# A GraphSAGE layer with sorted edges: nine buffers instead of five for the gathered leftover rows, and up to nine rows ahead

## The chip, the cores and the metric

The kernel runs on one core of a Trainium2 chip. The core has five engines with a queue each, which work side by side and wait for each other by semaphores: TensorE (PE in the profile, PEld for its weight loads), VectorE (DVE), ScalarE (ACT), GpSimd (POOL) and SyncE (SP, which here only issues transfers). Every engine takes its own instructions strictly in the order in which they stand. A transfer (DMA) is issued by an engine and then runs by itself.

The metric is the device time of one execution in microseconds (us), taken as the median of several runs. Less is better.

## What is computed

One layer of a graph network over 12500 nodes and 800000 random edges, 64 features each: every node sums the features of its neighbours, scales the sum, and two small weight matrices are applied.

```python
N, deg, D = 12500, 64, 64
E = N * deg
...
nsum = _segment_sum(x[src], dst, N)
h_neigh = nsum * deg_inv[:, None]
return x @ w_self + h_neigh @ w_neigh
```

`src` and `dst` are the two ends of each edge, drawn at random.

## The kernel before

The kernel sorts the edges itself. Each edge becomes one 32-bit key, made of its destination group, its source block of 128 nodes and the places inside both. The keys are sorted in 128 separate runs, one to a partition (DVE, line 230). Then rows of equal keys are cut out of the runs and merged, in two parts: part 0 holds the lower 37 buckets of each row, part 1 the upper 23. The cutting is done by `gather_runs` (line 394): one indirect DMA of POOL for each of 128 runs, followed by one or two short memsets of POOL that only pass time (`pause`, line 307). The merge (`merge_runs`) works on the tile `u`. It takes the runs in blocks of 32; for each block its first step copies on ACT (line 421) and compares on DVE (line 416), and needs all gathers of that block; further steps are at line 456. The three blocks of part 1 are `(0, 2), (2, 1), (3, 1)`: runs 0 to 63, 64 to 95 and 96 to 127.

The second half of the program is `nodes`. It goes through 7644 buckets (blocks, counted by `b0`), eight to a tile, in the order of destination groups; six groups of 98 blocks make an octet of 588 blocks, which shares one pair of accumulators. For each tile:

- `one_hots` makes, for 28 blocks at a time, two matrices of zeros and ones on DVE, `ohs` for the sources (line 838, three buffers) and `ohd` for the destinations (line 841, five buffers), from the lists `slb` that SP loads;
- PE multiplies `ohs` with the features `xh`, which picks the source rows into `ct` (line 867); ACT, and DVE for some tiles, copy them to `xg` (lines 877 and 875);
- two tiles later PE multiplies `xg` with `ohd` into the accumulators (line 923, in `sums`).

A bucket holds at most 128 edges that way. The few edges that don't fit are the leftovers: 140 lists of 128 edges. `uses` gives for each list the block at which it is added in. In the first octet all eight lists are added near its end, at blocks 404, 428, 452 and so on to 572. `rest(b0)`, called ahead of each tile's sums, does up to three things:

- it issues the indirect DMA that gathers a list's 128 source rows into a buffer `lx` (line 887, on POOL; at most one for each call);
- it makes the list's one-hot matrix `ohl` (line 895, DVE), with five buffers and at most five ahead;
- it multiplies the two into the accumulators (line 903, PE) once the block is reached.

A row load may be placed when fewer than five loaded lists are unused at that point of the program, and when its use is at most 400 blocks away (160 from near the first octet's end on). The buffer of a new load is that of the list five places earlier, so POOL waits until PE has used it.

The order of all this is the order of the program's text: from `after_sort` on no scheduler moves anything. `sums_and_merge` steps through the tiles of `nodes` by a counter `n` and puts other work between them: at every third `n` one of the last 32 gathers of part 1 (`runs`, numbers 96 to 127); from `n` = 8 on steps of the merge, as many as an allowance of 420 ns a tile pays for. The last block of the merge, which needs those 32 gathers, is not begun before `n` = 100 (`RESUME`). When the merge is done, part 1 is searched and decoded, and its leftovers follow. At the end of each octet `finish` writes the output (DMA at line 994 on POOL's queue, after DVE at lines 992 and 993).

Of the kernel before, what the change touches and what calls it, by code (L numbers as in the profile page):

```python
# [13 lines left out]
FH = mybir.dt.float16  # L14
# [54 lines left out]
READY = 8  # L69
SLOT = 1250  # L70
OCT = 6
LEAST = 2 * HN * NDB
LEND = 14

# [187 lines left out]
class Kernel:  # L262
# [497 lines left out]
    def tail(self, mps):  # L760
# [25 lines left out]
        for c in range(n):  # L786
# [3 lines left out]
                in_offset=bass.IndirectOffsetOnAxis(ap=s[:, c:c + 1].bitcast(U32), axis=0))  # L790
        m = pool.tile([128, n, N - LEAST], FH, name="tm")
        for c in range(n):
            if c % 4 == 0:
                yield
            nc.vector.tensor_scalar(m[:, c], self.wide[:, :N - LEAST], z[:, c:c + 1], -float(LEAST),
                                    op0=OP.subtract, op1=OP.is_equal)
        yield
        yield
        yield
        ps = mps.tile([128, N - LEAST], F32, name="tps", tag="ct", bufs=3)  # L800
        for c in range(n):
            nc.tensor.matmul(ps, rows[:, c], m[:, c], start=c == 0, stop=c == n - 1)
        g = pool.tile([128, N - LEAST], F32, name="tg")
        nc.scalar.activation(g, ps, AF.Copy)
# [5 lines left out]
    def uses(self):  # L810


        out = []
        for o in range(0, NBID, OCT * NB):
            end = min(o + OCT * NB, NBID)
            here = []
# [27 lines left out]
    def nodes(self, pool, aps, mps):  # L844


        nc = self.nc
        source = self.one_hots(pool)
        ready = []
        pend = []  # L850
        late = []
        done = []
        acc = own = None
        uses = self.uses()
        picked, ohl = [], []
        turn = 0

        def gather(b0, cnt, vector):

            nonlocal turn  # L860
            ct = aps.tile([128, 1024], F32, name="ct", bufs=3)
            while len(ready) < min(cnt + AHEAD, NBID - b0):
                ready.extend(next(source))
            cols = ready[:cnt]
            del ready[:cnt]
            for i in reversed(range(cnt)):
                nc.tensor.matmul(ct[:, i * 128:(i + 1) * 128], cols[i][0],  # L867
                                 self.xh[:, (b0 + i) % NB].rearrange("p a f -> p (a f)"), start=True, stop=True)
            xg = pool.tile([128, 1024], FH, name="xg", bufs=7)
            if vector and len(ready) < min(8 + AHEAD, NBID - b0 - cnt):  # L870
                turn += 1
            else:
                vector = False
            if vector and turn % 2:
                nc.vector.tensor_copy(xg[:, :cnt * 128], ct[:, :cnt * 128])  # L875
            else:
                nc.scalar.activation(xg[:, :cnt * 128], ct[:, :cnt * 128], AF.Copy)  # L877
            return b0, xg, [d for _, d in cols]

        def rest(b0):  # L880

            early = 400 if b0 < OCT * NB - 160 else 160
            if len(picked) < self.used + 5 and len(picked) < len(uses) and uses[len(picked)][0] - early <= b0 \
                    and uses[len(picked)][1] in self.left:
                _, p, c, _, _ = uses[len(picked)]
                x = pool.tile([128, 128], FH, name="lx", bufs=5)
                nc.gpsimd.indirect_dma_start(  # L887
                    out=x, out_offset=None, in_=self.xt,
                    in_offset=bass.IndirectOffsetOnAxis(ap=self.left[p][1][:, c:c + 1], axis=0))
                picked.append(x)  # L890
                self.picked = len(done)
            if len(ohl) < len(picked) and len(ohl) < self.used + 5 and uses[len(ohl)][0] - 96 <= b0:
                _, p, c, first, end = uses[len(ohl)]
                m = pool.tile([128, 4 * HN], FH, name="ohl", bufs=5)
                nc.vector.tensor_scalar(m[:, :(end + 1 - first) * 2 * HN], self.wide[:, :(end + 1 - first) * 2 * HN],
                                        self.left[p][0][:, c:c + 1], -float(first * 2 * HN),
                                        op0=OP.subtract, op1=OP.is_equal)
                ohl.append(m)
            while self.used < len(uses) and uses[self.used][0] <= b0:
                _, p, c, first, end = uses[self.used]  # L900
                m = ohl[self.used].rearrange("p (b h n) -> p b h n", h=2, n=HN)
                for h in range(2):
                    nc.tensor.matmul(acc[h][:, first % OCT * HN:(first % OCT + end + 1 - first) * HN],  # L903
                                     picked[self.used], m[:, :end + 1 - first, h], start=False, stop=False)
                self.used += 1

        def sums(job):

            nonlocal acc
            b0, xg, cols = job  # L910
            o = b0 // (OCT * NB)
            end = min((o + 1) * OCT * NB, NBID)
            last = b0 + len(cols) == end
            nb = min(OCT, NDB - o * OCT)
            width = nb * HN
            if b0 % (OCT * NB) == 0:
                acc = [aps.tile([128, OCT * HN], F32, name=f"acc{h}", bufs=1) for h in range(2)]
            rest(b0)
            for i, d in enumerate(cols):
                db, sb = divmod(b0 + i, NB)  # L920
                for h in range(2):
                    r = slice(h * H, (h + 1) * H)
                    nc.tensor.matmul(acc[h][:, db % OCT * HN:(db % OCT + 1) * HN], xg[r, i * 128:(i + 1) * 128], d[r],  # L923
                                     start=db % OCT == 0 and sb == 0, stop=b0 + i + 1 == end)
            if last:
                g = self.fin.tile([128, OCT, 2, HN], F32, name="g", bufs=1)
                for h in range(2):
                    nc.scalar.activation(g[:, :nb, h], acc[h][:, :width].rearrange("p (b n) -> p b n", n=HN), AF.Copy)
                g = g.rearrange("p b h n -> p (b h n)")
                for q in range(2):  # L930
                    if (2 * o + q) * 4 * FB < N:
                        late.append([b0 + 40 * (1 + 3 * q), self.finish(2 * o + q, g[:, q * 4 * FB:(q + 1) * 4 * FB],
                                                                        self.fin, mps, self.w2n, own and own[q])])
            return last

        tiles = []
        for o in range(0, NBID, OCT * NB):
            end = min(o + OCT * NB, NBID)
            tiles += [(b0, min(8, end - b0)) for b0 in range(o, end, 8)]
        for t, (b0, cnt) in enumerate(tiles):  # L940
            pend.append(gather(b0, cnt, t >= SHARE))
            if t % 2:
                while len(pend) > 2:
                    if sums(pend.pop(0)):
                        break
            if late and b0 >= late[0][0]:
                if next(late[0][1], self) is self:
                    late.pop(0)
                else:
                    late[0][0] = b0 + 40  # L950
            if t == len(tiles) - 12:
                own = [self.load_own(NQ - 3 + q, self.fin) for q in range(2)]
            done.append(t)
            yield t
        for job in pend:
            sums(job)
        for _, f in late:
            for _ in f:
                pass
# [270 lines left out]
```

## Time and profile before

| What | us |
| --- | --- |
| median of 3 runs | 1882.71 |
| lowest and highest run | 1881.04, 1889.39 |
| the profiled execution's time | 1888.32 |
| its span in the profile | 1886.6 |
| DVE busy | 1667.2 (88%) |
| ACT busy | 1169.7 (62%) |
| PE busy | 980.7 (52%) |
| POOL busy | 809.9 (43%) |
| POOL's row loads (line 887), 140 of them | 231.2 busy, 261.6 idle before them |
| POOL's gathers of runs (line 394), 256 of them | 374.0 busy, 178.8 idle before them |

How to read the rows of the profile that follow. A row of the timeline gives the start in us, the length in us, the engine, the line, the operation, what it writes and reads, how many instructions are merged in the row, and in brackets how long the engine stood idle before it and what ended that ("issue" where nothing that the profile shows did). A row of the waits says which instruction waited for which, with the sum in us, the number of times and the longest. A row of the stretches gives the window, its length, the busy time of each engine with the number of instructions, the granted clock of PE (1.00 is full), the busy share of the DMA engines and GB/s.

### The profile page before, as it was taken

How to read it: one execution, taken by the hardware profiler on the slowest of the kernel's cores; microseconds unless marked ns; L12 is line 12 of the kernel's file. 1: busy time of each engine (PE TensorE's matmuls, PEld its weight loads, DVE VectorE, ACT ScalarE, POOL GpSimd, SP SyncE). 2: the span in 40 equal slices, each digit the busy share in tenths (PEclk: the TensorE clock that was granted, in tenths of full speed). 3: DMA queues.
4: the chain of work that ended last, by engine and by line, in shares of the span. 5: the costliest groups of instructions: out<-in, count | busy, mean ns of one | idle time of the engine just before them, and what ended most of it. 6: DMA issues, size and time to landing. Idle time of an engine off the chain costs nothing.

```text
span 1886.6 us, 54681 instructions
## 1 busy us (share of the span) xinstructions
PE 980.7 (52%) x23698; PEld 839.0 (44%) x23698; DVE 1667.2 (88%) x1805; ACT 1169.7 (62%) x1868; POOL 809.9 (43%) x917
## 2 busy tenths in 40 slices
PE   0015100000000000185888888888868989988997
PEld 0003100000000000174777777777757778777886
DVE  6999999999559999797799999998897888888885
ACT  7435128206500032485898888889977877877786
POOL 1000000798889986888713131313552142222321
PEclk9998655555555555598899999999999999999999
DMA  4304100011100012476678877779766888788784
GB/s 153 70 0 100 36 32 7 21 35 38 22 19 9 10 45 79 127 267 194 211 228 240 264 238 262 244 253 329 264 203 228 267 274 264 253 277 254 247 261 144
DMA packets 104805, 305.25 MB, mean 162 GB/s; under 512 B 52945, under 2 KB 60491, under 8 KB 103915
## 3 DMA queue, kind: packets, MB, share of 16 engines
q1 hardware_dynamic: 86347, 277.44, 41.7%
q0 software_dynamic: 17632, 22.17, 8.8%
q8 instruction: 187, 3.06, 0.6%
q10 hardware_dynamic: 576, 2.07, 0.3%
q14 instruction: 63, 0.52, 0.1%
HBM read 282.20 MB, written 19.41 MB: 160 GB/s over the span
## 4 chain that ended last, share of the span: by engine, by line
DVE 42%; PE 25%; POOL 13%; issue 10%; ACT 5%; DMA 4%; DVEq 0%; SPq 0%; ACTq 0%; POOLq 0%
DVE u L456 15%; PE ct L867 13%; POOL u L394 10%; PE acc L923 9%; DVE b L230 6%; DVE a L230 6%; DVE ohd L841 6%; DVE ohs L838 4%; DMA slb<-sl 2%; ACT xg L877 2%; POOL pad L307 2%; POOL lx L887 1%; DVE u L416 1%; PE acc L903 1%; POOL v L620 1%
## 5 line engine op out<-in xcount | busy, mean ns | idle before, releaser
L877 ACT ACTIVATE xg<-ct 128x1024 f16<-128x1024 f32 (+1 forms) x898 | 852.2, 1033 | 187.3 <-PE ct L867 154.8
L867 PE MATMUL ct<-xh,ohs 128*128 128x128 f16 x7644 | 545.4, 224 | 80.3 <-DVE ohs L838 40.0
L867 PEld LDWEIGHTS <-ohs 128*128 128x128 f16 x7644 | 450.2, 100 | 125.6 <-issue 64.2
L394 POOL DMA_INDIRECT u<-d,ix x256 | 374.0, 1461 | 178.8 <-DVE ix L386 135.4
L923 PE MATMUL acc<-ohd,xg 64*128 64x80 f16 x15288 | 405.9, 199 | 64.2 <-issue 48.9
L456 DVE TENSOR_TENSOR u<-u 128x1456 f32<-128x1456 f32 (+51 forms) x314 | 398.1, 1291 | 19.7 <-ACT u L421 13.6
L923 PEld LDWEIGHTS <-xg 64*128 64x128 f16 x15288 | 319.7, 96 | 135.0 <-issue 65.2
L841 DVE TENSOR_TENSOR ohd<-iota,dlT 128x2240 f16<-128x2240 bf16 x273 | 359.8, 1318 | 0.0
L838 DVE TENSOR_SCALAR ohs<-slb,pidx 128x3584 f16<-128x3584 bf16 x273 | 314.7, 1153 | 35.1 <-PE ct L867 16.6
L887 POOL DMA_INDIRECT lx<-xt,lsrc x140 | 231.2, 1652 | 261.6 <-PE acc L903 228.4
L230 DVE TENSOR_TENSOR b<-a 128x608 f32<-128x608 f32 (+44 forms) x124 | 173.8, 1444 | 6.3 <-ACT a L232 2.3
L230 DVE TENSOR_TENSOR a<-b 128x608 f32<-128x608 f32 (+44 forms) x124 | 173.9, 1445 | 4.5
L994 POOL DMA_DIRECT2D out<-o x25 | 23.7, 949 | 339.6 <-DVE o L993 257.6
L384 PE MATMUL stp<-idf,st 128*128 128x128 f32 x2 | 0.9, 445 | 310.7 <-DVE st L382 310.7
L677 PE MATMUL tr<-idb,l 128*128 128x128 bf16 x60 | 8.0, 273 | 263.9 <-ACT l L671 253.2
L384 PEld LDWEIGHTS stp<-idf,st 128*128 128x128 f32 x2 | 0.4, 183 | 311.1 <-issue 311.1
L875 DVE CAST xg<-ct 128x1024 f16<-128x1024 f32 x64 | 78.2, 1223 | 68.3 <-PE ct L867 63.5
L677 PEld LDWEIGHTS <-l 128*128 128x128 bf16 x60 | 4.9, 117 | 267.1 <-ACT l L671 255.7
L421 ACT ACTIVATE u<-u 128x96 f32<-128x96 f32 (+36 forms) x155 | 32.9, 258 | 134.3 <-DVE u L456 71.1
L375 ACT ACTIVATE junka<-b,c 128x132 bf16<-128x132 f32 (+46 forms) x205 | 90.8, 443 | 12.3 <-DVE b L230 5.8
L232 ACT ACTIVATE b<-a 128x1 f32<-128x1 f32 (+21 forms) x52 | 18.7, 379 | 128.1 <-DVE a L230 122.2
L620 POOL DMA_INDIRECT v<-d,ix x60 | 73.8, 1230 | 55.5 <-ACT ix L638 46.1
(160 smaller groups left out, 795.5 us busy)
## 6 DMA issues: line engine op xcount, KB each, us to landing
slb<-sl SPq DMA_DIRECT2D x273, 896.0 KB
u<-d,ix POOLq DMA_INDIRECT x256
xt<-xh SPq DMA_DIRECT2D x1, 3136.0 KB
fo<-own SPq DMA_DIRECT2D x26, 120.0 KB
own<-os SPq DMA_DIRECT2D x12, 256.0 KB
out<-o POOLq DMA_DIRECT2D x24, 120.0 KB
lx<-xt,lsrc POOLq DMA_INDIRECT x140
rd<-dst SPq DMA_DIRECT2D x4, 521.0 KB
```

Source lines behind the costliest of these rows:

```text
L230: nc.vector.tensor_tensor(view(dst, lo + sh, [[st, g], [1, l]]), x, y, op=op)
L375: nc.scalar.activation(junks[0][:, :n], w, AF.Sign, bias=self.c1[:, 0, c:c + 1], accum_out=a)
L394: nc.gpsimd.indirect_dma_start(out=u[:nr, EDGE + p * w:EDGE + (p + 1) * w], out_offset=None, in_=src, in_offset=bass.IndirectOffsetOnAxis( ...
L456: nc.vector.tensor_tensor(view(dst, EDGE + o + out, d), view(src, EDGE + o + x, d), view(src, EDGE + o + x + gap, d), op=op)
L620: self.nc.gpsimd.indirect_dma_start(out=self.v[:, k].bitcast(F32), out_offset=None, in_=flat(self.d2[home(part, k)], 128 * PITCH2[home(par ...
L838: nc.vector.tensor_scalar(s.rearrange("p c s -> p (c s)"), b, self.pidx[:, :1], None, op0=OP.is_equal)
L841: nc.vector.tensor_tensor(d, self.iota[:, None].to_broadcast([128, 14, HN, 2]), ix, op=OP.is_equal)
L867: nc.tensor.matmul(ct[:, i * 128:(i + 1) * 128], cols[i][0], self.xh[:, (b0 + i) % NB].rearrange("p a f -> p (a f)"), start=True, stop=True)
L875: nc.vector.tensor_copy(xg[:, :cnt * 128], ct[:, :cnt * 128])
L877: nc.scalar.activation(xg[:, :cnt * 128], ct[:, :cnt * 128], AF.Copy)
L887: nc.gpsimd.indirect_dma_start(out=x, out_offset=None, in_=self.xt, in_offset=bass.IndirectOffsetOnAxis(ap=self.left[p][1][:, c:c + 1], ax ...
L923: nc.tensor.matmul(acc[h][:, db % OCT * HN:(db % OCT + 1) * HN], xg[r, i * 128:(i + 1) * 128], d[r], start=db % OCT == 0 and sb == 0, stop ...
```

## The change

Two numbers become one constant: how many lists may be loaded and not yet used, and how many buffers `lx` has. Both were 5 and are 9. The limit and the buffers of `ohl` stay at five.

```diff
 OCT = 6
+ROWAHEAD = 9
...
-            if len(picked) < self.used + 5 and len(picked) < len(uses) and uses[len(picked)][0] - early <= b0 \
+            if len(picked) < self.used + ROWAHEAD and len(picked) < len(uses) and uses[len(picked)][0] - early <= b0 \
                     and uses[len(picked)][1] in self.left:
                 _, p, c, _, _ = uses[len(picked)]
-                x = pool.tile([128, 128], FH, name="lx", bufs=5)
+                x = pool.tile([128, 128], FH, name="lx", bufs=ROWAHEAD)
```

The order of POOL's instructions changes in one place, in the first octet. The rows on PE, DVE, ACT and SP stand as they did. Here is POOL before, from the third and fourth row load on (`lx`); `u` is the gather of runs for part 1, `pad` the memsets behind it:

```order
L887 DMA lx<-xt,lsrc_2825 128x128 x2
L394 DMA u<-d_1_61,ix_1561 128x48
L307 MEMSET pad 128x95 x2
L887 DMA lx<-xt,lsrc_2825 128x128
L394 DMA u<-d_1_61,ix_1561 128x48
L307 MEMSET pad 128x95 x2
...
L887 DMA lx<-xt,lsrc_2825 128x128 x2
L394 DMA u<-d_1_61,ix_1561 128x48
L307 MEMSET pad 128x95 x2
```

Between the fifth load and the sixth and seventh stand twelve gathers with their memsets, of which the first is shown. The same place in the changed program, whose lines are counted one higher (888 is the row load, 395 the gather, 308 the memset):

```order
L888 DMA lx<-xt,lsrc_2825 128x128 x2
L395 DMA u<-d_1_61,ix_1561 128x48
L308 MEMSET pad 128x95 x2
L888 DMA lx<-xt,lsrc_2825 128x128 x3
L395 DMA u<-d_1_61,ix_1561 128x48
L308 MEMSET pad 128x95 x2
L395 DMA u<-d_1_61,ix_1561 128x48
L308 MEMSET pad 128x95 x2
L888 DMA lx<-xt,lsrc_2825 128x128
```

The sixth and seventh load now follow the fifth at once, the eighth and ninth come after two gathers each, and the gathers that stood ahead of them come later. The tenth load moves forward too, the eleventh and all later ones keep their places among POOL's instructions. The second place is the end of the gathers, on POOL in the changed program:

```order
L888 DMA lx<-xt,lsrc_2825 128x128
L395 DMA u<-d_1_61,ix_1561 128x48
L308 MEMSET pad 128x95 x2
L395 DMA u<-d_1_61,ix_1561 128x48
L308 MEMSET pad 128x95 x2
L995 DMA out<-o 120x4x64
L395 DMA u<-d_1_61,ix_1561 128x48
L308 MEMSET pad 128x95 x2
L888 DMA lx<-xt,lsrc_2825 128x128
L395 DMA u<-d_1_61,ix_1561 128x48
L308 MEMSET pad 128x95 x2
```

It begins with the eleventh load, and its last gather is the last one of part 1. These rows stand in the same order before, and the number of loads ahead of the last gather, twelve, is the same.

## The prediction, made before the changed kernel was run

> **What bounds the kernel now.** I read the waits of the whole span first, then the chain that ended last, then the timelines of PE, POOL, DVE and ACT between 815 and 980 us, then a table of stretches. The execution that was profiled and the rows that name the changed operation:
>
> ```profile
> span 1886.6 us, 54681 instructions
> POOL lx L887 <- PE acc L903: 228.4, 58, 10.2
> PE acc L903 <- DMA lx<-xt,lsrc: 14.9, 1, 14.9
> ```
>
> Two waits could be what more buffers remove. In the first, POOL holds a row load until PE has used the row five places earlier (a buffer comes free): 228.4 us in 58 waits. That is large, but it is POOL's idle time. In the second, PE waits for a row that has not landed: one wait only, 14.9 us. PE never waits for such a row again, so the 58 waits on POOL delay no load that anyone needs. The one PE wait is the whole direct prize. Here it is, with what POOL did at that time:
>
> ```profile
> 872.79 1.25 PE L867 MATMUL ct<-xh,ohs 128*128 128x128 f16 x16
> 888.92 0.45 PE L903 MATMUL acc<-ohl,lx 128*128 128x160 f16 x2 [14.88 <-DMA lx<-xt,lsrc]
> ...
> 858.72 2.45 POOL L887 DMA_INDIRECT lx<-xt,lsrc  x1 [0.15 <-issue]
> 861.47 2.75 POOL L394 DMA_INDIRECT u<-d,ix  x1 [0.30 <-issue]
> ...
> 866.73 1.64 POOL L394 DMA_INDIRECT u<-d,ix  x1 [0.15 <-issue]
> ...
> 882.40 0.95 POOL L394 DMA_INDIRECT u<-d,ix  x1 [0.15 <-issue]
> 883.93 0.95 POOL L394 DMA_INDIRECT u<-d,ix  x1 [0.16 <-issue]
> 885.84 0.95 POOL L887 DMA_INDIRECT lx<-xt,lsrc  x1 [0.53 <-issue]
> 887.10 0.94 POOL L887 DMA_INDIRECT lx<-xt,lsrc  x1 [0.30 <-issue]
> ...
> 907.93 4.37 POOL L394 DMA_INDIRECT u<-d,ix  x1 [0.15 <-issue]
> ...
> 925.87 1.86 POOL L394 DMA_INDIRECT u<-d,ix  x1 [0.31 <-issue]
> ```
>
> The sixth row load (885.84) did not wait for a buffer: its idle time is 0.53 us, "issue". It stood behind twelve gathers of runs (L394) in POOL's queue, because the program could only place it once the first of five rows had been used. And POOL is never idle from 861 to 928: every bracket here is 0.15 to 0.53 us. So the reader should ask who else waits for POOL at the end of this stream. DVE and ACT do:
>
> ```profile
> 892.79 0.69 DVE L456 TENSOR_TENSOR u<-u 128x510 f32<-128x510 f32 x1 [11.03 <-ACT u L421]
> 898.42 1.15 DVE L838 TENSOR_SCALAR ohs<-slb,pidx 128x3584 f16<-128x3584 bf16 x1 [4.94 <-remote]
> ...
> 926.83 1.32 DVE L841 TENSOR_TENSOR ohd<-iota,dlT 128x2240 f16<-128x2240 bf16 x1
> 931.90 1.28 DVE L416 TENSOR_TENSOR u<-u 128x656 f32<-128x656 f32 x1 [3.75 <-DMA lx<-xt,lsrc]
> ...
> 931.84 0.59 ACT L421 ACTIVATE u<-u 128x112 f32<-128x112 f32 x2 [2.29 <-DMA lx<-xt,lsrc]
> ```
>
> At 931.9 the merge of part 1 takes up its last block (runs 96 to 127). It needs the last gather, issued at 925.87. The view names lx, since it puts a wait for several DMAs down to the one that came last; L416 reads only u, so the gather is what it needs. This is a **second gate**, and DVE already waits 3.75 us at it. The stretches around both gates:
>
> ```profile
> 846.00:874.00 28.00, 23.67 (x594) 20.08 (x593) 28.00 (x34) 24.04 (x33) 24.88 (x27) 1.00 0.78 247
> 874.00:889.00 15.00, 0.12 (x2) 0.09 (x2) 7.55 (x10) 3.07 (x5) 12.53 (x24) 0.58 0.58 195
> 889.00:904.00 15.00, 12.29 (x192) 9.82 (x194) 4.85 (x6) 7.31 (x11) 12.06 (x22) 0.62 0.30 78
> 904.00:932.00 28.00, 25.75 (x662) 22.64 (x660) 20.03 (x23) 23.93 (x34) 22.17 (x25) 1.00 0.76 253
> 932.00:980.00 48.00, 42.44 (x1062) 36.22 (x1062) 47.44 (x53) 43.54 (x63) 13.27 (x8) 0.96 0.72 219
> 980.00:1140.00 160.00, 132.56 (x3484) 115.84 (x3485) 159.62 (x148) 140.64 (x166) 40.91 (x22) 1.00 0.78 245
> ```
>
> Columns: us, then busy time of PE, PE's weight loads, DVE, ACT, POOL, then the granted PE clock. POOL is full up to 932; from 932 on DVE is (47.44 of 48, 159.62 of 160). So whatever moves the start of L416 moves the rest of the program, and nothing ahead of it does.
>
> **The change, part by part.** *What moves.* By the order of the programs, row loads 6 to 10 come forward on POOL, the sixth past twelve gathers. Up to the last gather POOL holds the same instructions in both programs, and the rows on PE, DVE, ACT and SP keep their order. Later loads keep their places among POOL's rows, because there a row is placed at most 160 blocks ahead of its use.
>
> *What it removes.* The sixth row now leaves at about 861.5 and has landed long before PE asks at 874.0. PE's 14.88 us go, and with them DVE's 11.03 and 4.94. The slow clock after the stall goes from this place too: 889 to 904 shows 192 matmuls in 15 us, 12.8 a us, where 904 to 932 shows 662 in 28, 23.6 a us; at that rate the 192 take 8.1 us, so 6.9 are saved. DVE then reaches the second gate at 874.0 + (928.1 - 888.9) - 6.9 = 906.3 instead of 928.1.
>
> *Where the stall goes: the gathers.* From 861.5 on POOL has 25 gathers, 7 row loads and one output store up to the last gather's end. With DVE busy a gather and its two memsets take (882.40 - 866.73) / 8 = 1.96 us, and a row load about 2.3, the mean of these three and the 2.75 from 858.72 to 861.47:
>
> ```profile
> 846.11 2.12 POOL L887 DMA_INDIRECT lx<-xt,lsrc  x1 [0.96 <-DVE ohl L895]
> 848.53 2.62 POOL L887 DMA_INDIRECT lx<-xt,lsrc  x1 [0.30 <-issue]
> ...
> 853.30 1.36 POOL L887 DMA_INDIRECT lx<-xt,lsrc  x1 [0.15 <-issue]
> 854.96 1.24 POOL L887 DMA_INDIRECT lx<-xt,lsrc  x1 [0.31 <-issue]
> ```
>
> (2.42 and 1.66 from start to start.) With DVE idle they take 1.53 (882.40 to 883.93) and 1.26 (885.84 to 887.10). The store counts 2.0 and 1.2, an estimate between the two kinds. All with DVE busy: 25 x 1.96 + 7 x 2.3 + 2.0 = 67.1 us. All with DVE idle: 25 x 1.53 + 7 x 1.26 + 1.2 = 48.3. Before: 16.0 us of idle DVE (11.03 + 4.94) do 16.0 / 48.3 = 0.33 of the stream, the other 0.67 takes 44.9, together 60.9, which ends at 922.4; measured it ends at 925.87 + 1.86 + 0.43 for the memsets = 928.2, so 5.8 us are in slow single instructions such as the 4.37 at 907.93. After: DVE is busy to 906.3, 44.8 / 67.1 = 0.67 of the stream; the other 0.33 runs beside a waiting DVE in 16.1 us and ends at 922.4. The same: the idle time of DVE that helps POOL isn't removed, it only comes later. Between all of the 5.8 us coming back and none of them, I take half: the stream ends 2.9 us earlier (0 to 5.8).
>
> The landing may gain too: from the end of issue, 931.9 - 927.7 = 4.2 us before, but the row at 885.84 with DVE idle landed 888.9 - 886.8 = 2.1 us after its end. 0 to 2.1, I take 1.0. So L416 starts 3.9 us earlier (0 to 7.9), and DVE's wait there grows from 3.75 to about 22 us.
>
> The rows say 1.96 against 1.53 us for POOL beside a busy DVE. The Trainium skill, SBUF — State Buffer, section "SBUF: two separate sides", speaks against any load moved under a busy DVE: an instruction of DVE in a mode that takes the port pair it shares with GpSimd locks GpSimd out of writing descriptors until it ends. The trace agrees in sign only: rows of 1.24 to 1.64 us stand beside a DVE that is 28.00 of 28.00 busy, less than the 1.15 + 1.32 = 2.47 us of one pair of one-hot instructions.
>
> *The clock.* PE now stands from about 907 to 928 and restarts slowly at the second gate. By the row 889 to 904 that is 15 x (1 - 0.62) = 5.7 us of PE work. DVE is full there, not PE, and it may work ahead while one-hot buffers are free: one group of them is (from start to start)
>
> ```profile
> 942.22 1.14 DVE L838 TENSOR_SCALAR ohs<-slb,pidx 128x3584 f16<-128x3584 bf16 x1
> ...
> 946.13 1.15 DVE L838 TENSOR_SCALAR ohs<-slb,pidx 128x3584 f16<-128x3584 bf16 x1
> ```
>
> 3.9 us. I count one free group of the three: 5.7 - 3.9 = 1.8 us shown (0 to 5.7). The Trainium skill, TensorE: Matmul & The Clock Gate, section "What's actually happening", has the gate open after one busy window of some 3.4 us; by that PE would lose 3.4 x 0.5 = 1.7 us, all covered, and the sum would be -3.9. The trace's 15 us at 0.62 disagree, and I go by them.
>
> *Later rows.* POOL's 228.4 us of waiting shrink, at no gain: no row is late there. If some other cover went, the price would show as a PE wait at L903, of which there is none after 889. The four more buffers cost memory alone.
>
> **Sum**: -3.9 + 1.8 = -2.1 us, bounds -7.9 and +5.7. The profiled execution took 1888.32 us, 1.72 around its span of 1886.6; it becomes about 1886.2. It is 5.6 above the median of 1882.71, to which I apply the same difference: **1880.6 us**, by the bounds 1874.8 to 1888.4.
>
> **Rivals.** *A, the stall is paid out in full.* If POOL ran the moved stream at idle prices, it would end at 861.5 + 48.3 = 909.8, land at 911.9, and L416 would start 20 us earlier: less 1.8, 1864.5. For it: gathers of 0.95 us exist. Against it: they stand only where DVE is idle, and DVE is busier now. Something between, 10 to 15 us, would need gathers near 1.53 us from 861 on.
>
> *B, slower: the gathers choke.* Before, ten gathers and five row loads fell into 882.4 to 907.9, 25.5 us, mostly beside an idle DVE. Now DVE works, and POOL has worse rows beside it:
>
> ```profile
> 823.48 2.94 POOL L394 DMA_INDIRECT u<-d,ix  x1 [0.15 <-issue]
> 827.00 2.92 POOL L394 DMA_INDIRECT u<-d,ix  x1 [0.15 <-issue]
> 830.50 2.84 POOL L394 DMA_INDIRECT u<-d,ix  x1 [0.15 <-issue]
> ```
>
> That is 3.5 us each. 10 x 3.5 + 5 x 2.75 = 48.8, or 23.3 more. The seven instructions and the store after them gain, 5 x 1.53 + 2 x 1.26 + 1.2 = 11.4 for 20.3, so 8.9 back, and the landing 2.1: +12.3, with the clock's 1.8 +14.1, 1896.8. It decides from about 2.6 us a gather on, where 10 x 2.6 + 5 x 2.3 eats up what the end gives back. Against it: 1.96 us is the price nearest in time, with the same merge beside it. The port rule above, taken strictly, leads here: 0.95 and a whole pair of 2.47 are 3.4 us.
>
> *C, the change does nothing*: the sixth row is as late as before, because something else holds it (its buffer, its index). Then 1882.7. Against it: its buffer is new and the five loads ahead use the same index.
>
> **Chances.** The moved stall 0.66, A and its middle 0.16, B 0.12, C 0.06. What a measurement of this kernel can tell from no change is about 0.5%, 9.4 us: 1873.3 to 1892.1. Faster takes A and a little of the first, 0.20; slower takes B and a little, 0.14; the rest, 0.66, is within. The likeliest case's own range is 1874.8 to 1888.4; runs of before differ by 8 us, and the range reaches towards A and B: 1867 to 1892.
>
> **What would show it.** In the new profile PE's wait for lx should be gone (under 1 us), the sixth row load at about 862, DVE's wait before its L416 at 20 us or so with L416 between 924 and 932, PE's clock low from there for some 15 us, and POOL's wait for L903 far below 228. I am wrong if L416 starts before 920 or after 936, or if the time differs while L416 doesn't move.

## The result: slower by 0.7%, lost in the last part

The changed kernel takes 1895.5 us in the median of 9 runs (1892.9 to 1904.38), the kernel before 1882.89 in 9 runs on the same chip (1877.62 to 1889.39). The ratio, taken over all runs, is 1.0073, with a 95% interval from 1.0052 to 1.0094 (the two medians alone give 1.0067). The profiled execution took 1892.97 us, 2.5 under its median; that of before, 1888.32, lay 5.4 above its own. So the two profiles stand only 4.7 us apart where the medians stand 12.6 apart, and a single pair of them must be read with care.

The page of the changed kernel has, for the row loads (line 888 now) and for the output stores on the same queue:

```profile
L888 POOL DMA_INDIRECT lx<-xt,lsrc x140 | 223.8, 1599 | 109.6 <-PE acc L904 70.9
L995 POOL DMA_DIRECT2D out<-o x25 | 22.8, 910 | 499.5 <-DVE o L994 391.1
```

The row of the stores on the page of the kernel before:

```profile
L994 POOL DMA_DIRECT2D out<-o x25 | 23.7, 949 | 339.6 <-DVE o L993 257.6
```

POOL waited 228.4 us for buffers before and waits 70.9 now. Instead it now waits longer ahead of its output stores (499.5 us for 339.6).

The two gates of the first octet, in the timelines of POOL, DVE and PE of the changed kernel, with the only wait of PE for a row that the whole execution still has:

```profile
855.70 1.63 POOL L888 DMA_INDIRECT lx<-xt,lsrc  x1 [0.30 <-issue]
...
913.99 0.95 POOL L888 DMA_INDIRECT lx<-xt,lsrc  x1 [0.53 <-issue]
...
922.99 0.94 POOL L395 DMA_INDIRECT u<-d,ix  x1 [0.30 <-issue]
...
907.83 1.32 DVE L842 TENSOR_TENSOR ohd<-iota,dlT 128x2240 f16<-128x2240 bf16 x1
925.61 1.28 DVE L417 TENSOR_TENSOR u<-u 128x656 f32<-128x656 f32 x1 [16.46 <-DMA u<-d,ix]
...
917.06 0.45 PE L904 MATMUL acc<-ohl,lx 128*128 128x160 f16 x2 [5.50 <-DMA lx<-xt,lsrc]
```

The sixth row load leaves at 855.70 instead of 885.84. The last gather is issued at 922.99 instead of 925.87, and the last block of the merge (line 417 now) begins at 925.61 instead of 931.90, after a wait of 16.46 us that the view now puts down to the gather. Up to here this execution is 6.3 us ahead. PE's wait of 14.88 us is gone, but PE now waits 5.50 us for a later row, the one loaded at 913.99. It is the eleventh load, which kept its place behind the gathers (913.26 before) while PE came to it earlier. DVE has nothing to do from 909.15 to 925.61 but to wait for the last gather, so in this execution PE's wait holds nothing else up. The stretches around the restart, with the busy times of PE, PEld, DVE, ACT and POOL, then PE's clock:

```profile
925.00:932.00 7.00, 4.96 (x108) 4.48 (x110) 6.36 (x9) 6.40 (x10) 1.31 (x2) 0.63 0.32 96
932.00:939.00 7.00, 6.60 (x178) 5.86 (x174) 7.00 (x8) 5.93 (x9) 5.78 (x5) 1.00 0.88 210
```

Now follow DVE by its instructions, which are the same 1805 in both programs. Compared instruction by instruction, with the times of the kernel before as the scale, the changed kernel is 5.2 us ahead at 992 us, 10.5 ahead at 1399 us (near the end of the decoding of part 1), and then loses it: 0.9 behind at 1542 us, 10 behind at 1715 us, 4.7 at the end. The last 455 of DVE's instructions take 498.1 us instead of 482.9. That is 15.2 us, and it is where the time goes. The view of the waits over this last part, before (1400 to 1887 us; sum, number of times, longest):

```profile
POOL lx L887 <- PE acc L903: 138.0, 43, 9.7
POOL out L994 <- DVE o L993: 132.0, 9, 29.5
ACT xg L877 <- PE ct L867: 95.2, 110, 3.7
...
PEld L923 <- issue: 33.7, 41, 2.9
PE acc L923 <- issue: 24.5, 25, 2.8
```

and of the changed kernel (1390 to 1892 us):

```profile
POOL out L995 <- DVE o L994: 203.4, 9, 47.7
ACT xg L878 <- PE ct L868: 114.0, 110, 5.8
POOL lx L888 <- PE acc L904: 70.9, 16, 11.2
PEld L924 <- issue: 50.1, 40, 4.5
PE acc L924 <- issue: 42.6, 23, 4.4
```

ACT waits longer for PE (114.0 against 95.2), and PE waits for nothing that the profile shows: its "issue" grows from 24.5 to 42.6 us in as many waits, so each is longer. No wait for `lx` is among them. So in this last part PE is late, but not for the rows.

**What PE stands for.** One pair of places shows it, the same instructions in both programs. Before:

```profile
1779.03 0.30 PE L903 MATMUL acc<-ohl,lx 128*128 128x160 f16 x2
1779.27 0.76 PE L923 MATMUL acc<-ohd,xg 64*128 64x80 f16 x32
1779.96 1.07 PE L867 MATMUL ct<-xh,ohs 128*128 128x128 f16 x16
```

Changed:

```profile
1782.64 0.30 PE L904 MATMUL acc<-ohl,lx 128*128 128x160 f16 x2
1782.88 0.21 PE L924 MATMUL acc<-ohd,xg 64*128 64x80 f16 x1
1786.59 1.00 PE L924 MATMUL acc<-ohd,xg 64*128 64x80 f16 x31 [3.51 <-issue]
```

A group of 32 matmuls is cut after the first by a stop of 3.51 us. The page counts a DMA queue "instruction" with 187 packets of 16 KB (3.06 MB), and PE has 47430 records, nearly all of them matmuls and weight loads, so about one packet to 254 of them. Laid beside each other, the two lists give a rule: PE stops just before its record 256 k + 449, where k is the number of the packet (from 0), and it goes on 2.2 to 2.5 us after that packet has started (in a few cases up to 4.5). Where the packet starts early enough there is no stop. Here k is 165: before, that packet started at 1775.63 and PE passed the place without a stop; in the changed kernel it started at 1784.19, and PE, out of instructions at 1783.1, went on at 1786.6, 2.4 us later. The stops are PE's own program coming late.

What was under way ahead of it, on POOL before:

```profile
1758.50 0.84 POOL L994 DMA_DIRECT2D out<-o  x1 [17.04 <-DVE ohd L841]
1759.65 1.29 POOL L887 DMA_INDIRECT lx<-xt,lsrc  x1 [0.30 <-issue]
...
1765.48 1.43 POOL L887 DMA_INDIRECT lx<-xt,lsrc  x1 [0.30 <-issue]
1769.05 2.25 POOL L887 DMA_INDIRECT lx<-xt,lsrc  x1 [2.14 <-PE acc L903]
1779.61 1.15 POOL L887 DMA_INDIRECT lx<-xt,lsrc  x1 [8.30 <-PE acc L903]
```

and in the changed kernel:

```profile
1762.98 0.84 POOL L995 DMA_DIRECT2D out<-o  x1 [9.15 <-DVE ohd L842]
1764.13 1.29 POOL L888 DMA_INDIRECT lx<-xt,lsrc  x1 [0.30 <-PE ct L868]
...
1771.67 1.63 POOL L888 DMA_INDIRECT lx<-xt,lsrc  x1 [0.30 <-issue]
1773.60 1.61 POOL L888 DMA_INDIRECT lx<-xt,lsrc  x1 [0.30 <-DMA lx<-xt,lsrc]
1775.52 0.94 POOL L888 DMA_INDIRECT lx<-xt,lsrc  x1 [0.30 <-issue]
1776.77 0.94 POOL L888 DMA_INDIRECT lx<-xt,lsrc  x1 [0.30 <-issue]
1778.02 0.94 POOL L888 DMA_INDIRECT lx<-xt,lsrc  x1 [0.30 <-issue]
1783.22 2.76 POOL L888 DMA_INDIRECT lx<-xt,lsrc  x1 [4.26 <-PE acc L904]
```

The store stands in POOL's queue ahead of the loads and holds them until DVE has made the output. Behind it five buffers let four loads go at once and a fifth after 2.14 us; nine let nine go without a pause (1764 to 1779), 1.25 to 2.3 us apart from start to start. The DMA queues in the ten microseconds ahead of that place (packets, MB, share of 16 engines), before (1770 to 1780):

```profile
q1 hardware_dynamic: 426, 2.75, 67.6%
q0 software_dynamic: 63, 0.05, 6.4%
```

and changed (1774 to 1784):

```profile
q0 software_dynamic: 158, 0.17, 52.9%
q1 hardware_dynamic: 304, 1.91, 49.2%
```

The packets of the row gathers (q0, POOL's) add up to half of the time of 16 engines for 0.17 MB; how much of a packet's time is waiting, the profile doesn't say.

### The profile page after: what moved, and what is told of

The parts are those of the page before. It is cut to its first block, busy times and chain, and to the rows that moved or that the text cites. A ratio compares the mean times of both kernels' runs of the same rounds, so it can differ in the third digit from the quotient of the medians.

```text
span 1891.2 us, 54691 instructions
## 1 busy us (share of the span) xinstructions
PE 974.6 (52%) x23698; PEld 838.7 (44%) x23698; DVE 1667.4 (88%) x1805; ACT 1170.3 (62%) x1868; POOL 799.0 (42%) x917
## 3 DMA queue, kind: packets, MB, share of 16 engines
q8 instruction: 187, 3.06, 0.7%
## 4 chain that ended last, share of the span: by engine, by line
DVE 42%; PE 24%; issue 13%; POOL 11%; ACT 5%; DMA 4%; DVEq 0%; SPq 0%; ACTq 0%; POOLq 0%
DVE u L457 15%; PE ct L868 13%; PE acc L924 9%; POOL u L395 9%; DVE ohd L842 6%; DVE b L231 6%; DVE a L231 6%; DVE ohs L839 4%; ACT xg L878 2%; POOL pad L308 2%; DMA slb<-sl 1%; DVE u L417 1%; DMA rd<-dst 1%; PE po L987 1%; PE acc L904 1%
## 5 line engine op out<-in xcount | busy, mean ns | idle before, releaser
L395 POOL DMA_INDIRECT u<-d,ix x256 | 368.3, 1439 | 178.9 <-DVE ix L387 135.4
L888 POOL DMA_INDIRECT lx<-xt,lsrc x140 | 223.8, 1599 | 109.6 <-PE acc L904 70.9
L995 POOL DMA_DIRECT2D out<-o x25 | 22.8, 910 | 499.5 <-DVE o L994 391.1
```

Of the source, the lines that this page charges most:

```text
L395: nc.gpsimd.indirect_dma_start(out=u[:nr, EDGE + p * w:EDGE + (p + 1) * w], out_offset=None, in_=src, in_offset=bass.IndirectOffsetOnAxis( ...
L888: nc.gpsimd.indirect_dma_start(out=x, out_offset=None, in_=self.xt, in_offset=bass.IndirectOffsetOnAxis(ap=self.left[p][1][:, c:c + 1], ax ...
```

## The experiments

After the result two theories stood against each other. **Bursts**: the later loads, let go back to back, disturb the fetch of PE's instructions. **Phase**: the last part is slower because it is reached earlier, or with other places in memory, whatever the later loads do. The edits are against the changed kernel, except in the last one. The first four kernels shared 31 runs of the kernel before with median 1887.33, the last four 26 runs with 1885.12; their runs scatter more than in the first comparison (1871.56 to 1899.29 and 1872.03 to 1895.94, where it was 1877.62 to 1889.39).

**Nine in the first octet alone.** The first ten lists have nine buffers, all later ones five of their own.

```diff
-            if len(picked) < self.used + ROWAHEAD and ...
+            if len(picked) < self.used + (ROWAHEAD if len(picked) < 10 else 5) and ...
-                x = pool.tile([128, 128], FH, name="lx", bufs=ROWAHEAD)
+                x = pool.tile([128, 128], FH, name="lx", bufs=ROWAHEAD) if len(picked) < 10 \
+                    else pool.tile([128, 128], FH, name="ly", bufs=5)
```

> Nine buffers and nine rows ahead for the first ten lists alone; all later lists have five buffers of their own and the limit of five. Theory T (later, loads that POOL issues in unbroken bursts make PE's 16 KB instruction fetches late): the gain at the second gate stays (L417 some 6 us earlier than before) and the loss of some 15 us behind 1400 us goes; 1873 to 1879 us. Rival P (the loss comes from the program reaching its last part earlier, with PE, its fetches and the big loads falling differently together): as slow as the change, 1890 to 1900.

1884.41 us, ratio 0.9994 (0.9958 to 1.003). The loss is gone, so it does not come from the first octet. The gain that was expected below the kernel before is not seen.

**Nine buffers, five ahead.** The limit goes back to five, and with it the order of POOL's instructions; the buffers stay nine.

```diff
-            if len(picked) < self.used + ROWAHEAD and ...
+            if len(picked) < self.used + 5 and ...
```

> Nine buffers, but the limit of five rows ahead, so POOL's order is that of before. T: PE's 14.9 us wait in the first octet is back, and the late loads still run freely; the loss behind 1400 us without the gain, 1893 to 1903 us. P: nothing arrives earlier, so the time of before, 1880 to 1886.

1896.1 us, ratio 1.005 (1.0014 to 1.0086). The loss is there (0.5%, between 0.14 and 0.86) although the first octet stands as before, with its stall. In its profile the last part begins later than before, at 1403 us for 1399, and still takes 13.6 us more; so the loss does not come from reaching it early. In its waits:

```profile
POOL lx L888 <- PE acc L904: 66.5, 18, 9.8
PE acc L904 <- DMA lx<-xt,lsrc: 14.6, 1, 14.6
```

**Nine ahead, five buffers.** The other half of the change.

```diff
-                x = pool.tile([128, 128], FH, name="lx", bufs=ROWAHEAD)
+                x = pool.tile([128, 128], FH, name="lx", bufs=5)
```

> POOL's order of the change with five buffers: the sixth load waits for the first row's use, which comes at 855 us, so it still leaves at about 862. T: gain kept, late loads held back as before, 1873 to 1879 us. P: 1890 to 1900. If the place of the buffers in memory were the cause, 1873 to 1879 too.

1887.12 us, ratio 1.0006 (0.9969 to 1.0043): no loss. POOL's waits for a buffer are back:

```profile
POOL lx L888 <- PE acc L904: 222.4, 56, 9.6
```

These two together say that the number of buffers makes the loss and the order does not. Their intervals overlap a little (1.0014 to 1.0043); the eighteen buffers below bear it out.

**Nine, but paced.** The changed kernel, with six short memsets of POOL behind each load after the first octet, which only pass time (about 1.4 to 2.3 us for the six). The loads then stand 2.8 us or more apart from start to start, less than expected.

```diff
+                if b0 >= OCT * NB:
+                    self.pause(6)
```

> The change, with six short memsets on POOL (some 0.58 us each) behind every row load from the second octet on, so that loads of a burst stand 4 to 5 us apart instead of 1.3 to 1.9. T: the fetches recover at least in part, 1875 to 1888 us. P: no better than the change, 1890 or more.

1885.48 us, ratio 1.0 (0.9967 to 1.0034). The buffers are nine, their places in memory those of the changed kernel, and the loads as early as POOL's queue lets them; only the gap between them is new, and the loss is gone. This speaks against the theory of the phase and against the places in memory, and for the bursts. PE's longest stop at its sums falls to 2.5 us (from 4.5):

```profile
PEld L926 <- issue: 32.7, 34, 2.5
```

**The changed kernel again**, as a measure beside the next three.

> The changed kernel once more, for a comparison on one chip with the other three. Both theories: as measured, some 0.7% over before (0.5 to 0.9%).

1894.54 us, ratio 1.0065 (1.0036 to 1.0093).

**Three buffers later.** As the first experiment, with three in place of five.

```diff
+            if len(picked) < self.used + (ROWAHEAD if len(picked) < 10 else 3) and ...
+                    else pool.tile([128, 128], FH, name="ly", bufs=3)
```

> Nine buffers and nine ahead for the first ten lists, then three buffers and a limit of three. T (bursts of loads make PE's instruction fetches late): the bursts behind an output store get shorter still than with five; the last part, from the end of the merge on, takes no longer than before's 483 us in the profile, 465 to 483; the time 0 to 0.6% under before. A rival (five is right because rows with fewer buffers come late): PE waits for rows in many places, slower than before by over 0.3%.

1886.69 us, ratio 1.0008 (0.9981 to 1.0036). POOL now waits still longer for buffers, at no loss; the gain that was held possible is not seen:

```profile
POOL ly L889 <- PE acc L905: 339.0, 79, 11.9
```

**Eighteen buffers**, nine ahead.

```diff
-                x = pool.tile([128, 128], FH, name="lx", bufs=ROWAHEAD)
+                x = pool.tile([128, 128], FH, name="lx", bufs=18)
```

> The change with eighteen buffers and the limit of nine. T: every load behind a store leaves at once, seven in a row instead of five to nine cut by waits; at least as slow as the change, 0.7 to 1.2% over before. A rival (a matter of how nine buffers turn over, so that a load happens to fall on a fetch): no order by size, anywhere from 0 to 0.7%.

1910.1 us, ratio 1.0127 (1.009 to 1.0164), a little more than expected; the loads come in chains of up to 12, where seven were expected. POOL hardly waits for a buffer over the whole span, and PE's stops in the last part grow again (second row, from 1390 us on):

```profile
POOL lx L888 <- PE acc L904: 1.2, 4, 0.3
...
PEld L924 <- issue: 52.7, 47, 5.1
```

**Five, paced.** The kernel before, with the same memsets behind each later load.

> The kernel before, with six short memsets of POOL behind each load from the second octet on. T: the bursts of five are spread too; the last part takes 470 to 483 us, the time 0 to 0.6% under before. A rival (the memsets themselves made the paced change faster or slower, by the port POOL shares with DVE): over before by 0.3% or more.

1882.73 us, ratio 0.9998 (0.9967 to 1.0028). No loss, and not the gain that was held possible: bursts of five cost nothing that can be measured.

The ten profiled executions side by side, worked out from their traces. "In bursts" are row loads after 1400 us that stand in chains of four or more with less than 1 us between one's end and the next's start; "stops" is the sum of PE's stops of over 0.3 us just before its records 256 k + 449, from k = 100 on (from start to start of the two records, less the 0.1 us that is usual); "last part" is the time from DVE's instruction 1350 to the end of its program.

| kernel | in bursts | stops, us | last part, us | ratio to before |
| --- | --- | --- | --- | --- |
| before | 9 | 36.3 | 482.9 | 1 |
| five, paced | 0 | 37.5 | 472.9 | 0.9998 |
| nine, paced | 0 | 41.8 | 472.3 | 1.0 |
| nine in the first octet | 13 | 39.2 | 475.0 | 0.9994 |
| nine ahead, five buffers | 9 | 42.5 | 476.9 | 1.0006 |
| three later | 0 | 46.6 | 483.1 | 1.0008 |
| nine buffers, five ahead | 48 | 52.6 | 496.5 | 1.005 |
| changed, again | 49 | 50.3 | 490.2 | 1.0065 |
| changed | 47 | 53.5 | 498.1 | 1.0073 |
| eighteen buffers | 61 | 58.9 | 505.3 | 1.0127 |

The four executions with long bursts are those of the three slower kernels, and their stops, 50.3 to 58.9 us, lie above all the others' 36.3 to 46.6. One execution of each is little for the order inside the two groups. Between the first two profiles the stops grow by 17.2 us and the last part by 15.2.

## Why the prediction was wrong

The forecast was 1880.6 us, 2.1 less than before, in a range from 1867 to 1892; measured are 1895.5, 12.6 more than before.

**The step that failed** is the one on the later rows: "POOL's 228.4 us of waiting shrink, at no gain: no row is late there", costed at nothing, with the sentence that a lost cover would show as a PE wait at L903. The first half came true: 70.9 us, and behind the second gate PE waits for no row. But the waits did cover something: they spread the loads that stood behind an output store. The prediction asked only whether a row comes too late, not what nine of them do at once when they come early. That the buffers and nothing else of the change make the loss, and that a gap between the loads takes it away, is shown by the second, third, fourth and seventh experiment. That PE's stops are late instruction packets is shown by the traces; between the first two profiles the stops grow by 17.2 us and the last part by 15.2. The stops don't give the time of every single execution, though: five, paced, has nearly the stops of before and a last part 10.0 us shorter, three later has 10.3 us more of stops and the last part of before.

That it is the bursts that make the packets late is a reading of both together; no run delayed a packet in another way. The traces support it. In the last part no packet k of the ten executions starts more than 0.4 us before PE's record 256 k + 193, which is 256 records ahead of the place where PE stops for it, and these 256 records take PE 4.8 us (median). Counted from that record, a packet of the changed kernel starts 3.97 us later on average while a chain of four or more loads is going out or has ended less than 5 us ago (20 packets), and 2.01 us later otherwise (64). Starts over 5 us later number 6 to 8 in the four executions with long bursts and 1 to 3 in the other six. What holds the packet up stays open. Three buffers with no burst at all still had 46.6 us of stops, so bursts are not the only thing that moves them.

**The first gate** was right for the load, which moved from 885.84 to 855.70 (forecast about 862), and for the waits at that place, PE's and DVE's, which went. The sign "PE's wait for lx should be gone (under 1 us)" was not met: PE waits 5.5 us for the eleventh row. Together PE's waits for rows are 4.8 to 10.6 us in the seven executions with the new order of the first octet, and 14.6 to 15.2 in the three with the order of five.

**The second gate** was right in kind: the stall moved to DVE's wait ahead of the last merge block, 16.46 us for the forecast 22 (15.4 to 17.4 in the seven executions with the new order, 3.8 to 9.9 in the three with the old one). That this block began 6.3 us earlier, at 925.61, inside 924 to 932, for the forecast 3.9 (0 to 7.9), was luck for the most part. In this execution POOL's first row load, which nothing in the change moves, already stood 3.5 us earlier (842.63 for 846.11), DVE's instruction 780 only 0.8. From DVE's instruction 780 to that block (857.2 to 931.9 before) the three executions with the order of five took 74.7, 71.6 and 74.5 us, mean 73.6; the seven with the new order 69.2, 70.5, 73.3, 76.6, 74.4, 68.7 and 71.5, mean 72.0. The two shortest are the two in which the first row load stood 13.8 us ahead of DVE's instruction 780; in the eight others it stood 11.1 ahead. Without these two the mean of the new order is 73.3. So a gain at this gate is not shown, and the changed kernel itself gave 5.5 us against the 74.7 in one execution and 0.3 in the other. This fits the kernels that kept the new order and lost the bursts: they did not come out faster.

**The clock** was low only for a short time behind the second gate. PE went on at 927.04; the clock was 0.50 ahead of that, 0.63 from 925 to 932 and 1.00 from 932 to 939. Taken as half and then full, it rose at 925 + 7 x (1 - 0.63) / 0.5 = 930.2, so 3.1 us at half speed, 1.6 us of PE's work, where the prediction took 5.7. The row that it went by, 0.62 from 889 to 904, was no single slow restart: there the clock was 0.50 from 889 to 893, 1.00 from 894 to 896.5 and 0.50 again from 897 to 903.5. No price shows behind the gate: from that block to DVE's instruction 1350 the changed kernel took 462.9 us, before 467.1.

**Rivals.** A, the stall paid out in full, fell: the block began 6.3 us earlier, not 20. B, choking gathers, fell too: the last gather was issued 2.9 us earlier, not later. Its sign was right, for another reason. C fell. Of the two signs of being wrong that the prediction gave, neither came as it stands: L416 lay between 920 and 936, and it did move. The loss came behind it, in a part for which the prediction had no sign but a wait for rows.

## What to carry to other kernels

A queue's wait for a free buffer may be what spaces its transfers; before taking it away, look at what stands ahead of those transfers in the same queue (here a store that waits for another engine) and ask how many will leave at once when it goes. When an engine's waits named "issue" grow, compare their places with the packets of the DMA queue "instruction". If the early rows are wanted for one place, give that place the buffers and leave the rest, or space the rest.

## What the hardware showed that was not expected

PE's instructions come as DMA packets of 16 KB, one to 256 of its records, and PE can stand for them: 36.3 us of stops in the last part already before the change, up to 4.4 us for one packet after it. A packet that came late in both kernels (k = 164) started at 1769.68 and 1774.22, and PE went on 2.2 and 2.3 us later.

The packets of the row gathers take long for their size when many are under way. In the 10 us shown, POOL's 158 packets were 75 of 4 bytes, 9 ns each, and 83 of 2 KB, 1.01 us each; before, in the matching 10 us, 26 of 2 KB took 0.38 us each. SP's packets of 7 KB beside them took 0.29 us in the changed kernel and 0.28 us before. These are the packets' times in the profile; how much of them is waiting is not shown.
